# Talking-heads attention and two MoE layers on one core: pre-mix and post-mix as matmuls in two array halves of 64 columns

## The chip, the core and the metric

The kernel runs on one NeuronCore of one Trainium2 chip. Its engines work side by side, each through its own instruction stream: PE (TensorE) multiplies, with its weight loads shown as PEld; DVE (VectorE), ACT (ScalarE) and POOL (GpSimd) work element by element; SP (SyncE) only issues DMAs. The metric is the device time of one execution in microseconds. A **record** is one PE instruction in the trace: a float32 matmul of this kernel leaves two records, each with a weight load of its own.

## The reference, cut to what matters

```python
# q, k, v: (4, 12, 448, 64); w_pre, w_post: (12, 12)
scores = scale * np.matmul(q, k.transpose(0, 1, 3, 2))
scores = np.einsum('bhij,hg->bgij', scores, w_pre)          # pre-mix over heads
scores = scores - np.max(scores, axis=-1, keepdims=True)
attn = np.exp(scores)
attn = attn / (np.sum(attn, axis=-1, keepdims=True) + 1e-09)
attn = np.einsum('bhij,hg->bgij', attn, w_post)             # post-mix over heads
attn_out = np.matmul(attn, v)                               # AV
x = attn_out.transpose(0, 2, 1, 3).reshape(1792, 768)
# two MoE layers follow: 768 -> 1024 (SoLU and a norm) -> 768, then 768 -> 2048 (ReLU squared) -> 768
```

## The kernel before, in words

The attention takes each of the 4 batches in 4 chunks of queries (120, 120, 120 and 88). Each chunk is cut into blocks of at most 10 queries (R = 10), 180 blocks in all. With 12 heads a block has up to 120 (query, head) rows, and these are the partitions on which the mixes over heads work:

- `qk` (L199) makes the scores of one chunk, a third of the heads at a time, with 64 contracted rows in either row half of the array, and writes them to `ssrc`.
- `shuffle` (L214) is a DMA that lays the scores of a block out as 120 (query, head) rows by 448 keys, `sdst`.
- `pre` (L226) is the pre-mix: one matmul of a 120x120 block-diagonal matrix `wpre_bd` with the 448 columns of `sdst`. `negmax` (DVE, L239) and `expo` (ACT, L251) follow.
- `weigh` (every second block) turns the sums into `w`: DVE adds and takes the reciprocal (L260, L262), POOL multiplies the block-diagonal post weights by it (L268). For the last 14 blocks ACT does this (L275).
- `post` (L288) is the post-mix: for each of 4 pieces of 112 keys one matmul with `e` (120x112) as weights and `w` (120 columns) streaming. It turns the block so that keys are the partitions. `post_out` (DVE, L302) copies the 480 elements per partition to `at`.
- `av` (L315) runs once for a finished chunk: for 6 pairs of heads and 4 pieces of keys, two matmuls with 64 weight columns, one for each head, which write to PSUM partitions 0 to 63 and 64 to 127: the two column halves of the array. ACT copies the result to `xt` (L325, L330); `x_out` (L340) stores it.

The order on every engine is written out by hand: one loop over slots `s`, one slot for a block, issues `shuffle(s+8)`, `pre(s+3)`, `post_out(s-1)`, `weigh(s+1)`, `negmax` and `expo(s+3)`, any `qk` and `av` that is due, and last `post(s)`. So PE's order in a slot is pre, qk or av if there is one, post. Other work is spread over the slots: splitting q and k into high and low parts, narrowing the first MoE weights (`filler`), and late in the attention the loads for the first MoE layer (`prep_first`) and four pieces of its first matmuls (L419). The MoE layers that follow are untouched by the change.

## Time and profile before

| | |
|---|---|
| device time, 3 executions | 1178.35, 1180.03 and 1181.02 us; median 1180.03 us |
| profiled execution's own time (its span, first to last instruction) | 1178.6 us |
| PE busy | 1168.5 us, 99% |
| PE weight loads busy | 1021.1 us, 87% |
| DVE, ACT, POOL busy | 744.8, 490.9, 279.8 us |
| granted TensorE clock | 1.00 over the whole span (the upper level, 2.4 GHz) |

PE counts as busy from the start of a record to its modelled end, and the records overlap in the array, so a busy PE says little by itself. What a matmul costs is read from the distance between the starts of neighbouring rows in the timeline.

### The profile page before, as it was taken

How to read it: one execution, taken by the hardware profiler on the slowest of the kernel's cores; microseconds unless marked ns; L12 is line 12 of the kernel's file. 1: busy time of each engine (PE TensorE's matmuls, PEld its weight loads, DVE VectorE, ACT ScalarE, POOL GpSimd, SP SyncE). 2: the span in 40 equal slices, each digit the busy share in tenths (PEclk: the TensorE clock that was granted, in tenths of full speed). 3: DMA queues.
4: the chain of work that ended last, by engine and by line, in shares of the span. 5: the costliest groups of instructions: out<-in, count | busy, mean ns of one | idle time of the engine just before them, and what ended most of it. 6: DMA issues, size and time to landing. Idle time of an engine off the chain costs nothing.

```text
span 1178.6 us, 21505 instructions
## 1 busy us (share of the span) xinstructions
PE 1168.5 (99%) x8034; PEld 1021.1 (87%) x8034; DVE 744.8 (63%) x1480; ACT 490.9 (42%) x1206; POOL 279.8 (24%) x386
## 2 busy tenths in 40 slices
PE   9999999999999999999999999999999999999998
PEld 4777777777777768899899999999999999999998
DVE  4776777677777664853354378457676767676734
ACT  4556555666666554422122146533232222222211
POOL 2342223223322161730110074211111111111100
PEclk9999999999999999999999999999999999999999
DMA  6875766566656452411110265212121212121113
GB/s 178 215 200 166 224 185 193 164 216 202 185 179 195 137 172 86 121 48 48 54 41 27 70 200 173 69 41 64 45 62 46 65 44 63 45 66 43 41 68 121
DMA packets 103267, 134.40 MB, mean 114 GB/s; under 512 B 21499, under 2 KB 86395, under 8 KB 103163
## 3 DMA queue, kind: packets, MB, share of 16 engines
q1 hardware_dynamic: 102379, 132.75, 37.7%
q8 instruction: 64, 1.05, 0.4%
q14 instruction: 40, 0.33, 0.1%
q10 hardware_dynamic: 784, 0.27, 0.1%
HBM read 71.65 MB, written 22.81 MB: 80 GB/s over the span
## 4 chain that ended last, share of the span: by engine, by line
PE 91%; DVE 2%; DMA 2%; ACT 1%; issue 1%; POOL 1%; SPq 0%; POOLq 0%; DVEq 0%; ACTq 0%
PE ps_y L885 19%; PE ps_h L846 19%; PE ps_post L288 12%; PE ps_pre L226 10%; PE ps_h L419 10%; PE ps_o L692 8%; PE ps_av L315 6%; PE ps_qk L199 6%; PE ps_tr L678 1%; DMA x2r<-x2D 1%; DMA wraw<-w1iD 1%; DMA wr<-in_moe_w_out_dram 1%; DVE nm L239 1%; DVE at L302 0%; ACT e L251 0%
## 5 line engine op out<-in xcount | busy, mean ns | idle before, releaser
L846 PE MATMUL ps_h<-x,ti 128*128 128x384 f32 (+1 forms) x1440 | 241.6, 325 | 0.0
L885 PE MATMUL ps_y<-to,g 128*128 128x384 f32 x1332 | 239.3, 336 | 1.1 <-ACT y L894 1.1
L846 PEld LDWEIGHTS ps_h<-x,ti 128*128 128x128 f32 x1440 | 236.6, 188 | 0.0
L885 PEld LDWEIGHTS ps_y<-to,g 128*128 128x128 f32 x1332 | 231.0, 188 | 3.4 <-DVE y L896 1.9
L288 PEld LDWEIGHTS ps_post<-w,e 120*112 120x112 f32 (+1 forms) x1440 | 168.3, 177 | 68.4 <-issue 48.2
L302 DVE COPY at<-ps_post 112x480 f32<-112x480 f32 x180 | 117.3, 652 | 109.4 <-PE ps_post L288 108.9
L288 PE MATMUL ps_post<-w,e 120*112 120x120 f32 (+1 forms) x1440 | 182.7, 270 | 2.6 <-ACT w L275 2.1
L251 ACT ACTIVATE e<-ps_pre,nm 120x448 f32<-120x448 f32 x180 | 114.6, 637 | 132.0 <-POOL w L268 73.3
L226 PE MATMUL ps_pre<-sdst,wpre_bd 120*120 120x448 f32 x360 | 166.3, 545 | 0.8 <-ACT e L251 0.7
L854 ACT ACTIVATE r<-ps_h 128x384 f32<-128x384 f32 (+1 forms) x80 | 37.4, 468 | 213.1 <-PE ps_h L846 213.1
L692 PE MATMUL ps_o<-zt,w1o 128*128 128x384 f32 (+1 forms) x720 | 120.1, 326 | 0.0
L419 PE MATMUL ps_h<-w1i,xs 128*128 128x512 f32 x504 | 119.2, 393 | 0.4 <-ACT xt L330 0.4
L855 DVE SCALAR_TENSOR_TENSOR r<-ps_h,r 128x384 f32<-128x384 f32 (+1 forms) x80 | 42.4, 531 | 121.7 <-ACT r L854 121.7
L692 PEld LDWEIGHTS ps_o<-zt,w1o 128*128 128x128 f32 x720 | 117.0, 189 | 0.0
L239 DVE TENSOR_REDUCE nm<-ps_pre 120x1 f32<-120x448 f32 x180 | 110.2, 613 | 7.9 <-PE ps_pre L226 5.3
L896 DVE TENSOR_TENSOR y<-ps_y,y 128x768 f32<-128x768 f32 x97 | 92.4, 953 | 31.2 <-PE ps_y L885 31.2
L419 PEld LDWEIGHTS ps_h<-w1i,xs 128*128 128x128 f32 x504 | 93.9, 188 | 19.9 <-ACT xt L330 0.6
L268 POOL TENSOR_TENSOR w<-wpost_bd,sm 120x120 f32<-120x120 f32 x166 | 64.1, 406 | 188.1 <-DVE sm L262 176.8
L208 ACT COPY ssrc<-ps_qk 120x448 f32<-120x448 f32 (+1 forms) x186 | 84.9, 543 | 10.0 <-PE ps_qk L199 10.0
L315 PEld LDWEIGHTS ps_av<-at,v 112*64 112x64 f32 x1536 | 73.8, 137 | 11.4 <-ACT ssrc L208 5.3
L802 POOL TENSOR_TENSOR ti<-wt,ti 128x384 fp32r<-128x384 f32 x32 | 34.7, 1085 | 205.4 <-ACT ti L801 205.3
L315 PE MATMUL ps_av<-at,v 112*64 112x120 f32 (+1 forms) x1536 | 78.0, 261 | 0.4 <-ACT xt L325 0.3
(79 smaller groups left out, 1168.1 us busy)
## 6 DMA issues: line engine op xcount, KB each, us to landing
sdst<-ssrc SPq DMA_DIRECT2D x172, 210.0 KB
wr<-in_moe_w_in_dram SPq DMA_DIRECT2D x32, 384.0 KB
wr<-in_moe_w_out_dram SPq DMA_DIRECT2D x32, 384.0 KB
w1raw<-in_moe_w_in_dram SPq DMA_DIRECT2D x24, 256.0 KB
w1raw<-in_moe_w_out_dram SPq DMA_DIRECT2D x24, 256.0 KB
kraw<-in_kT_dram SPq DMA_DIRECT2D x24, 224.0 KB
v<-in_v_dram SPq DMA_DIRECT2D x16, 336.0 KB
out_dram<-y SPq DMA_DIRECT2D x13, 384.0 KB
```

The costliest lines, as they stand in the source:

```text
L208: (nc.vector.tensor_copy if dve else nc.scalar.copy)(ssrc[c][0:n, h, :], ps[0:n, 0:S])
L226: nc.tensor.matmul(out=ps[0:m, 0:S], lhsT=wpre_bd[0:m].rearrange("p i g -> p (i g)")[:, 0:m], rhs=d[0:m], start=True, stop=True,)
L239: nc.vector.tensor_reduce(out=nm[0:m], in_=ps[0:m, 0:S], op=ALU.max, axis=AX.X, negate=True)
L251: nc.scalar.activation(out=e[0:m], in_=ps[0:m, 0:S], func=AF.Exp, bias=nm[0:m], scale=1.0, accum_out=sm[0:m])
L288: nc.tensor.matmul(out=ps[:, j, :, 0:r], lhsT=e[0:m, j * JW:(j + 1) * JW], rhs=w[0:m, :, 0:r], start=True, stop=True,)
L302: nc.vector.tensor_copy(at[c][:, :, :, oa:oa + r], ps[:, :, :, 0:r])
L315: nc.tensor.matmul(out=ps[64 * e:64 * e + 64, 0:n], lhsT=vv[ch["b"], j][:, 2 * p + e], rhs=a[:, j, 2 * p + e, 0:n], start=(j == 0), stop=( ...
L419: nc.tensor.matmul(out=ps[:, u], lhsT=t[:, a, cc], rhs=w1i[cc][:, w, u * 512:(u + 1) * 512], start=(cc == 0 and a == 0 and w == 0), stop=( ...
L692: nc.tensor.matmul(out=ps[:, 0:width], lhsT=w1o[k][:, w, cc * 128:(cc + 1) * 128], rhs=zT[:, a, k, 0:width], start=(k == 0 and i == 0), st ...
L846: nc.tensor.matmul(out=ps[:, 0:n], lhsT=ti[:, w, cc, f * 128:(f + 1) * 128], rhs=x2[q][:, a, cc], start=(cc == 0 and i == 0), stop=(cc == ...
L885: nc.tensor.matmul(out=ps[:, u - us[0], 0:DM // 2], lhsT=g[:, a, f, o:o + 128], rhs=to[:, w, f, u * (DM // 2):(u + 1) * (DM // 2)], start= ...
L896: nc.vector.tensor_tensor(out=yo, in0=po, in1=yo, op=ALU.add)
```

## The change

The pre-mix is now eight matmuls for a block: four pieces of 112 keys (QP), each once for the first and once for the second half of the block's queries, with 64 weight columns (60 of them used) and results in PSUM partitions 0 to 63 or 64 to 127. So the 120 rows of a block lie on 128 partitions with a gap of 4 in each half, and `negmax`, `expo` and `weigh` work on 128 partitions. The post-mix cuts the keys into pieces of 64: three pairs of pieces, each piece in its own column half against all 120 columns of `w`, and a last piece of 64 keys that both halves take, one with heads 0 to 5, the other with heads 6 to 11 (60 columns each). `at` therefore holds 420 elements per partition for a block of ten queries, not 480. AV keeps its 8 matmuls for a pair of heads, now heads p and p+6. Its last piece contracts over 128 partitions that hold the same 64 keys twice, for either head, against a tile of V in which the other head's half is zero; POOL sets these zeros. The loads of V, the store of `xt` and the constants follow the new layout.

```diff
@@ -41,8 +41,14 @@
     R = 10
-    JW = 112
+    JW = 128
     NJ = S // JW
+    JL = S - NJ * JW
+    G2 = H // 2
+    NU = NJ * H + G2
+    RH = R // 2
+    PR = RH * H
+    QP = 112
...
     mask_sb = const.tile([120, R], F32, name="mask_sb")
-    wp_raw = const.tile([120, 2, H], F32, name="wp_raw")
-    wpre_bd = const.tile([120, R, H], F32, name="wpre_bd")
-    wpost_bd = const.tile([120, H, R], F32, name="wpost_bd")
+    mask_gap = const.tile([128, R], F32, name="mask_gap")
+    wp_raw = const.tile([120, H], F32, name="wp_raw")
+    wq_raw = const.tile([128, H], F32, name="wq_raw")
+    wpre_bd = const.tile([120, 2, 64], F32, name="wpre_bd")
+    wpost_bd = const.tile([128, H, R], F32, name="wpost_bd")
...
     def load_v(b, j):
-        t = late_p.tile([JW, H, D], F32, tag=f"v_{j}", name="v", bufs=2)
-        nc.sync.dma_start(out=t, in_=v[b, j * JW:(j + 1) * JW].rearrange("j (g d) -> j g d", g=H))
+        if j < NJ:
+            t = late_p.tile([JW, H, D], F32, tag=f"v_{j}", name="v", bufs=2)
+            nc.sync.dma_start(out=t, in_=v[b, j * JW:(j + 1) * JW].rearrange("j (g d) -> j g d", g=H))
+        else:
+            t = late_p.tile([128, 2, G2, D], F32, tag=f"v_{j}", name="v", bufs=2)
+            src = v[b, j * JW:S].rearrange("j (e g d) -> e j g d", e=2, g=G2)
+            for e in range(2):
+                nc.gpsimd.memset(t[64 - 64 * e:128 - 64 * e, e], 0.0)
+            for e in range(2):
+                nc.sync.dma_start(out=t[64 * e:64 * e + 64, e], in_=src[e])
         vv[b, j] = t
 
...
@@ -223,56 +239,50 @@
         m = blocks[t][2] * H
         d = sdst.pop(t)
         ps = psb_p.tile([128, 512], F32, tag="pre", name="ps_pre", bufs=2)
-        nc.tensor.matmul(
-            out=ps[0:m, 0:S],
-            lhsT=wpre_bd[0:m].rearrange("p i g -> p (i g)")[:, 0:m],
-            rhs=d[0:m],
-            start=True,
-            stop=True,
-        )
+        for o in range(0, S, QP):
+            for u in range(2):
+                nc.tensor.matmul(
+                    out=ps[64 * u:64 * u + 64, o:o + QP],
+                    lhsT=wpre_bd[0:m, u],
+                    rhs=d[0:m, o:o + QP],
+                    start=True,
+                    stop=True,
+                )
         pres[t] = ps
...
     def expo(t):
-        m = blocks[t][2] * H
         ps, nm = pres.pop(t)
-        e = late_p.tile([120, S], F32, tag="e", name="e", bufs=4)
+        e = late_p.tile([128, S], F32, tag="e", name="e", bufs=4)
         if t % 2 == 0:
-            sms[t] = late_p.tile([120, 2], F32, tag="sm", name="sm", bufs=4)
-            if m < 120 or blocks[t + 1][2] < R:
-                nc.vector.memset(sms[t], 1.0)
+            sms[t] = late_p.tile([128, 2], F32, tag="sm", name="sm", bufs=4)
         sm = sms[t - t % 2][:, t % 2:t % 2 + 1]
-        nc.scalar.activation(
-            out=e[0:m], in_=ps[0:m, 0:S], func=AF.Exp, bias=nm[0:m], scale=1.0, accum_out=sm[0:m]
-        )
+        nc.scalar.activation(out=e, in_=ps[:, 0:S], func=AF.Exp, bias=nm, scale=1.0, accum_out=sm)
         es[t] = e
...
     def weigh(t):
 
-        m = max(blocks[u][2] for u in (t, t + 1)) * H
         sm = sms.pop(t)
-        nc.vector.tensor_scalar(out=sm[0:m], in0=sm[0:m], scalar1=1e-9, scalar2=None, op0=ALU.add)
+        nc.vector.tensor_scalar(out=sm, in0=sm, scalar1=1e-9, scalar2=None, op0=ALU.add)
...
-            m = blocks[t + u][2] * H
-            w = late_p.tile([120, H, R], F32, tag="w", name="w", bufs=4)
+            w = late_p.tile([128, H, R], F32, tag="w", name="w", bufs=4)
             if t < tail:
                 nc.gpsimd.tensor_tensor(
-                    out=w[0:m].rearrange("p g i -> p (g i)"),
-                    in0=wpost_bd[0:m].rearrange("p g i -> p (g i)"),
-                    in1=sm[0:m, u:u + 1].to_broadcast([m, H * R]),
+                    out=w.rearrange("p g i -> p (g i)"),
+                    in0=wpost_bd.rearrange("p g i -> p (g i)"),
+                    in1=sm[:, u:u + 1].to_broadcast([128, H * R]),
                     op=ALU.mult,
                 )
             else:
-                nc.scalar.activation(out=w[0:m], in_=wpost_bd[0:m], func=AF.Copy, scale=sm[0:m, u:u + 1])
+                nc.scalar.activation(out=w, in_=wpost_bd, func=AF.Copy, scale=sm[:, u:u + 1])
...
 
     def post(t):
         r = blocks[t][2]
-        m = r * H
         e, w = es.pop(t), ws.pop(t)
-        ps = psa_p.tile([JW, NJ, H, R], F32, tag="post", name="ps_post", bufs=2)
-        for j in range(NJ):
-            nc.tensor.matmul(
-                out=ps[:, j, :, 0:r],
-                lhsT=e[0:m, j * JW:(j + 1) * JW],
-                rhs=w[0:m, :, 0:r],
-                start=True,
-                stop=True,
-            )
+        ps = psa_p.tile([128, NU, R], F32, tag="post", name="ps_post", bufs=2)
+        for j in range(NJ + 1):
+            for u in range(2):
+                o = j * JW + u * 64 if j < NJ else NJ * JW
+                g0, ng = (0, H) if j < NJ else (u * G2, G2)
+                nc.tensor.matmul(
+                    out=ps[64 * u:64 * u + 64, j * H:j * H + ng, 0:r],
+                    lhsT=e[:, o:o + 64],
+                    rhs=w[:, g0:g0 + ng, 0:r],
+                    start=True,
+                    stop=True,
+                )
         pps[t] = ps
 
     def post_out(t):
         c, k, r, oa = blocks[t]
         ps = pps.pop(t)
         if c not in at:
-            at[c] = late_p.tile([JW, NJ, H, 120], F32, tag="at", name="at", bufs=2)
-        nc.vector.tensor_copy(at[c][:, :, :, oa:oa + r], ps[:, :, :, 0:r])
+            at[c] = late_p.tile([128, NU, 120], F32, tag="at", name="at", bufs=2)
+        nc.vector.tensor_copy(at[c][:, :, oa:oa + r], ps[:, :, 0:r])
...
         ps = pool.tile([128, 512], F32, tag=tag, name="ps_av", bufs=bufs)
-        for j in range(NJ):
+        for j in range(NJ + 1):
+            t = vv[ch["b"], j]
             for e in range(2):
+                g = p + e * G2
                 nc.tensor.matmul(
                     out=ps[64 * e:64 * e + 64, 0:n],
-                    lhsT=vv[ch["b"], j][:, 2 * p + e],
-                    rhs=a[:, j, 2 * p + e, 0:n],
+                    lhsT=t[:, g] if j < NJ else t[:, e, p],
+                    rhs=a[:, j * H + (g if j < NJ else p), 0:n],
                     start=(j == 0),
-                    stop=(j == NJ - 1),
+                    stop=(j == NJ),
                 )
...
     def x_out(c, eng=nc.sync):
         ch = chunks[c]
         t0, n = ch["b"] * S + ch["i0"], ch["n"]
-        eng.dma_start(
-            out=xD[:, t0:t0 + n].rearrange("(c p) t -> p c t", p=128),
-            in_=xt.pop(c)[:, :, 0:n],
-        )
+        x = xt.pop(c)
+        for e in range(2):
+            eng.dma_start(
+                out=xD[e * G2 * D:(e + 1) * G2 * D, t0:t0 + n].rearrange("(c d) t -> d c t", d=D),
+                in_=x[64 * e:64 * e + 64, :, 0:n],
+            )
...
+    nc.gpsimd.memset(mask_gap, 0.0)
+    nc.gpsimd.memset(wq_raw, 0.0)
+    nc.gpsimd.memset(wpre_bd, 0.0)
     nc.sync.dma_start(out=mask_sb, in_=mask)
-    for u, w in enumerate((w_pre, w_post)):
-        nc.sync.dma_start(out=wp_raw[:, u, :], in_=w.unsqueeze(0).to_broadcast([R, H, H]))
+    nc.sync.dma_start(out=wp_raw, in_=w_pre.unsqueeze(0).to_broadcast([R, H, H]))
     load_q(1)
+    for u in range(2):
+        nc.sync.dma_start(out=mask_gap[64 * u:64 * u + PR], in_=mask[u * PR:(u + 1) * PR])
+        nc.sync.dma_start(out=wq_raw[64 * u:64 * u + PR], in_=w_post.unsqueeze(0).to_broadcast([RH, H, H]))
 
...
-        )
+        nc.vector.tensor_scalar(out=wp_raw, in0=wp_raw, scalar1=scale, scalar2=None, op0=ALU.mult)
+        for u in range(2):
+            nc.vector.tensor_tensor(
+                out=wpre_bd[:, u, 0:PR].rearrange("p (i g) -> p i g", g=H),
+                in0=wp_raw.unsqueeze(1).to_broadcast([120, RH, H]),
+                in1=mask_sb[:, u * RH:(u + 1) * RH].unsqueeze(2).to_broadcast([120, RH, H]),
+                op=ALU.mult,
+            )
         nc.vector.tensor_tensor(
             out=wpost_bd,
-            in0=wp_raw[:, 1, :].unsqueeze(2).to_broadcast([120, H, R]),
-            in1=mask_sb.unsqueeze(1).to_broadcast([120, H, R]),
+            in0=wq_raw.unsqueeze(2).to_broadcast([128, H, R]),
+            in1=mask_gap.unsqueeze(1).to_broadcast([128, H, R]),
             op=ALU.mult,
...
     for c, ch in enumerate(chunks):
         if ch["i0"] == 0:
-            for j in range(NJ):
+            for j in range(NJ + 1):
                 at_slot(ch["first"] + ([6, 8, 10, 12] if c == 0 else [0, 2, 4, 6])[j], load_v, ch["b"], j)
```

On PE, early in the attention, around the `av` of the first chunk. Before, the rows are (x4 means four matmuls in a row):

```order
L199 MATMUL ps_qk<-k,q 120x448 x12
L288 MATMUL ps_post<-w,e 112x120 x4
L226 MATMUL ps_pre<-sdst,wpre_bd 120x448
L288 MATMUL ps_post<-w,e 112x120 x4
L226 MATMUL ps_pre<-sdst,wpre_bd 120x448
L315 MATMUL ps_av<-at,v 64x120 x48
L288 MATMUL ps_post<-w,e 112x120 x4
```

At the same place on PE in the changed kernel:

```order
L215 MATMUL ps_qk<-k,q 120x448 x12
L300 MATMUL ps_post<-w,e 64x120 x6
L300 MATMUL ps_post<-w,e 64x60 x2
L244 MATMUL ps_pre<-sdst,wpre_bd 64x112 x8
L300 MATMUL ps_post<-w,e 64x120 x6
L300 MATMUL ps_post<-w,e 64x60 x2
L244 MATMUL ps_pre<-sdst,wpre_bd 64x112 x8
L329 MATMUL ps_av<-at,v 64x120 x48
L300 MATMUL ps_post<-w,e 64x120 x6
```

The sequence of steps is the same. A block's mixes are 16 matmuls where they were 5, each with 64 weight columns as in AV; qk and AV are the same matmuls as before.

On SP, from the start of the program, where the inputs are loaded. Before:

```order
L166 DMA qraw<-in_qT_dram 64x720 x2
L149 DMA kraw<-in_kT_dram 64x2x448 x6
L449 DMA mask_sb<-in_mask_dram 120x10
L451 DMA wp_raw<-in_w_pre_dram 120x1x12
L451 DMA wp_raw<-in_w_post_dram 120x1x12
L166 DMA qraw<-in_qT_dram 64x720 x2
L214 DMA sdst<-ssrc 120x1x448 x2
```

The same place on SP after the change:

```order
L174 DMA qraw<-in_qT_dram 64x720 x2
L157 DMA kraw<-in_kT_dram 64x2x448 x6
L468 DMA mask_sb<-in_mask_dram 120x10
L469 DMA wp_raw<-in_w_pre_dram 120x1x12
L174 DMA qraw<-in_qT_dram 64x720 x2
L472 DMA mask_gap<-in_mask_dram 60x10
L473 DMA wq_raw<-in_w_post_dram 60x1x12
L472 DMA mask_gap<-in_mask_dram 60x10
L473 DMA wq_raw<-in_w_post_dram 60x1x12
L230 DMA sdst<-ssrc 120x1x448 x2
```

One small load in front of the second load of q is gone, and four small ones stand behind it, ahead of the first shuffle.

On POOL, in the second batch, in the changed kernel (w is the weighted post matrix, v the last piece of V, k and q the splits):

```order
L278 TENSOR_TENSOR w<-wpost_bd,sm 128x120 x4
L194 MEMSET v 64x384 x2
L278 TENSOR_TENSOR w<-wpost_bd,sm 128x120 x6
L184 TENSOR_TENSOR q<-qraw,q 128x264
L278 TENSOR_TENSOR w<-wpost_bd,sm 128x120 x2
```

The two MEMSET rows are new, once in each of the 4 batches; the rows around them stand as before.

## Rows read from the trace of the kernel before

**Rows 1.** The page: engine totals, granted clock in 40 slices, chain that ended last.

```profile
PE 1168.5 (99%) x8034; PEld 1021.1 (87%) x8034; DVE 744.8 (63%) x1480; ACT 490.9 (42%) x1206; POOL 279.8 (24%) x386
...
PEclk9999999999999999999999999999999999999999
...
PE 91%; DVE 2%; DMA 2%; ACT 1%; issue 1%; POOL 1%; SPq 0%; POOLq 0%; DVEq 0%; ACTq 0%
```

**Rows 2.** Windows: us, busy us (instructions) of each engine, clock, DMA share, GB/s.

```profile
24.00:406.00 382.00, 381.37 (x3325) 282.78 (x3325) 276.91 (x720) 234.48 (x652) 112.21 (x208) 1.00 0.64 190
...
432.00:466.00 34.00, 32.65 (x332) 26.52 (x330) 16.37 (x40) 15.56 (x54) 11.53 (x16) 1.00 0.44 133
466.00:1179.00 713.00, 708.02 (x4084) 684.68 (x4084) 426.62 (x663) 215.67 (x438) 139.81 (x133) 1.00 0.23 69
```

**Rows 3.** Timeline of PE from 300 us: start, us, line, records, idle before.

```profile
300.65 0.92 PE L226 MATMUL ps_pre<-sdst,wpre_bd 120*120 120x448 f32 x2
301.50 5.14 PE L315 MATMUL ps_av<-at,v 112*64 112x120 f32 x96
306.57 1.07 PE L288 MATMUL ps_post<-w,e 120*112 120x120 f32 x8
307.48 0.92 PE L226 MATMUL ps_pre<-sdst,wpre_bd 120*120 120x448 f32 x2
308.24 0.98 PE L288 MATMUL ps_post<-w,e 120*112 120x120 f32 x8
309.06 0.92 PE L226 MATMUL ps_pre<-sdst,wpre_bd 120*120 120x448 f32 x2
309.90 1.46 PE L199 MATMUL ps_qk<-k,q 64*120 64x448 f32 x12
311.30 1.07 PE L288 MATMUL ps_post<-w,e 120*112 120x120 f32 x8
312.21 0.92 PE L226 MATMUL ps_pre<-sdst,wpre_bd 120*120 120x448 f32 x2
```

**Rows 4.** Timeline of ACT: copies of finished AV head pairs, chunk of 120 queries.

```profile
305.05 0.37 ACT L325 COPY xt<-ps_av 128x120 f32<-128x120 f32 x1 [0.45 <-PE ps_av L315]
305.87 0.37 ACT L325 COPY xt<-ps_av 128x120 f32<-128x120 f32 x1 [0.45 <-PE ps_av L315]
```

**Rows 5.** The same for a chunk of 88 queries.

```profile
136.60 0.29 ACT L325 COPY xt<-ps_av 128x70 f32<-128x70 f32 x1 [0.29 <-PE ps_av L315]
...
137.21 0.28 ACT L325 COPY xt<-ps_av 128x70 f32<-128x70 f32 x1 [0.29 <-PE ps_av L315]
```

**Rows 6.** The page's groups: xcount, busy us, mean ns, idle before and its releaser.

```profile
L302 DVE COPY at<-ps_post 112x480 f32<-112x480 f32 x180 | 117.3, 652 | 109.4 <-PE ps_post L288 108.9
L288 PE MATMUL ps_post<-w,e 120*112 120x120 f32 (+1 forms) x1440 | 182.7, 270 | 2.6 <-ACT w L275 2.1
...
L226 PE MATMUL ps_pre<-sdst,wpre_bd 120*120 120x448 f32 x360 | 166.3, 545 | 0.8 <-ACT e L251 0.7
```

**Rows 7.** Timeline of PE late in the attention.

```profile
434.40 1.07 PE L288 MATMUL ps_post<-w,e 120*112 120x120 f32 x8 [0.61 <-ACT w L275]
435.24 1.63 PE L419 MATMUL ps_h<-w1i,xs 128*128 128x512 f32 x6
436.71 0.92 PE L226 MATMUL ps_pre<-sdst,wpre_bd 120*120 120x448 f32 x2
```

**Rows 8.** Waits, whole span: who for whom, us in total, times, longest.

```profile
PEld ps_post L288 <- POOL w L268: 12.5, 34, 0.9
```

**Rows 9.** Timeline of the start: POOL and SP.

```profile
0.73 0.31 POOL L438 MEMSET wz<- 128x256 f32 x1 [0.29 <-POOLq L968]
...
6.66 0.90 SPq L451 DMA_DIRECT2D wp_raw<-in_w_pre_dram  x1
...
13.75 1.73 SPq L214 DMA_DIRECT2D sdst<-ssrc  x2
```

**Rows 10.** The page's DMA queues: packets, MB, share of 16 engines.

```profile
q8 instruction: 64, 1.05, 0.4%
```

15 lines of the change are left out of this document (3 added, 12 removed).

## Prediction, made before the changed kernel had run

> **What bounds the kernel now.** I read the page first, for the one engine that is never idle; then the windows, to cut the span into stretches; then PE's timeline inside the attention, because the page's busy time counts overlapping records. The page gives PE 99% of the span, the chain that ended last runs through PE for 91% of it, and the clock is at its upper level in every slice [rows 1]. In the windows the attention's steady part, 24 to 406 us, has PE busy for 381.4 of 382 us while DVE has 277, ACT 234 and POOL 112; after 466 us come the MoE layers, which the change does not touch [rows 2]. In PE's timeline the reader is to look at distances between starts: a post-mix takes 0.82 us (308.24 to 309.06), a pre-mix 0.76 (307.48 to 308.24), and the next step begins at once [rows 3]. PE's waits for data are 2.6 us before all post-mixes and 0.8 before all pre-mixes [rows 6]. So up to about 430 us the attention is as long as the sum of PE's steps, and a shorter step should shorten the span.
>
> There are 180 blocks [rows 6]. The sum below is made against the profiled execution's 1178.6 us; the median of the three runs is 1.4 us above that, and I add this at the end.
>
> **What a matmul in a column half costs.** The trace of before holds this form already, in AV: two halves of 64 weight columns. ACT's copies show when each pair of heads is done, and a pair of heads is 8 matmuls, 16 records, that is 8 times two records side by side. With 120 streaming columns a pair of heads takes 0.82 us (305.05 to 305.87) [rows 4], so two records side by side take 0.1025 us; a full-width post-mix record of the same 120 columns takes as long alone (0.82 us for 8 records) [rows 3]. With 88 columns it is 0.61 us, 0.076 us for two side by side [rows 5]. Between 88 and 120 columns the cost follows the columns (0.026 us for 32 of them, 0.83 ns each), so neither loading of weights nor issue shows at 88.
>
> **Post-mix.** It was 8 records, 0.82 us. Now there are three pairs of pieces with 120 columns: 6 times two records side by side, 0.615 us. The last piece has 60 columns, 2 times two records. By columns alone one such pair is 0.076 less 28 times 0.83 ns, 0.053 us. It can't be cheaper than that; if the 0.076 us at 88 columns is already the floor, it is 0.076. A weight load of 64 columns lies close by: after AV, where the first load can't be done ahead, the post-mix takes 0.91 instead of 0.82 us (306.57 to 307.48) [rows 3], 0.09 us for 112 columns, so about 0.052 for 64. I take 0.055, close to the columns' side, since at 88 the columns still rule. The post-mix is then 0.615 + 0.11 = 0.725 us, 0.095 less; times 180, **-17.1 us** (bounds -17.6 and -9.5).
>
> **Pre-mix.** It was 0.76 us by the row; its two records of 448 columns, at 0.83 ns each as below 120 columns in AV, would be 0.747; I take 0.755. Now 16 records of 112 columns, 8 times two side by side, each between the two AV rows: 0.076 + 24 times 0.83 ns = 0.096, in all 0.768 us. 0.013 more; times 180, **+2.3 us** (from 0 to +5, if the first records of each block don't close up). That both halves stream the same rows, where AV's stream different ones, no row shows; it is a rival below.
>
> **The changes of mode around AV.** Entering AV from the pre-mix costs 0.85 (300.65 to 301.50) where 0.755 is streaming: 0.09. AV takes 5.07 us (301.50 to 306.57) for 48 times 0.1025 = 4.92: 0.15. The post-mix behind it takes 0.91 for 0.82: 0.09 [rows 3]. Now pre-mix, AV and post-mix all work in the same two halves, and the three should vanish: 0.33 us at 15 of the 16 chunks (the last AV is followed by the MoE's matmuls), **-5.0 us** (0 if something else than the mode makes the gap).
>
> **The changes around qk** stay: qk still splits the array by rows. Only the load that lies open behind it is shorter, 64 columns for 112: the post-mix from 311.30 takes 0.91 [rows 3], and of its 0.09 us 0.04 goes. Of the 48 qk groups the three of the first chunk stand before any mix and two more run into another step; 43 stand ahead of a post-mix: **-1.7 us**. Four pieces of MoE matmuls (L419, full width) stand among the last blocks; today they follow without a seam (434.40 to 435.24, 0.84 us) [rows 7]. Each now gets two changes, about 0.19 going in and 0.15 coming out, by the seams above: **+1.5 us**.
>
> **What is hidden, and behind what.** The copy to `at` on DVE goes from 480 to 420 elements; it is 652 ns and its engine waits 108.9 us in all for the post-mix [rows 6]: a gain without effect. Two zero fills of 64x384 on POOL in each batch: the start's fill of 128x256 took 0.31 us [rows 9], so about 0.5 each, on an engine that is busy for 112 of 382 us [rows 2]. Behind them on POOL stand the products `w`, for which the post-mix waits; uncovered, all eight would cost 4 us, and I count nothing, since they wait for no new data and can run in POOL's idle time. SP gets a net of three small loads at the start: up to 0.90 us each, 2.7 us of issue. From the end of the row at 6.66 to the first shuffle at 13.75 the old queue has 6.2 us for three loads [rows 9]; six fit as well, so nothing. Later it gets one more issue for each store of `xt` and each last piece of V, again under 0.90 us each, on a queue that runs 8 slots ahead. The zero-padded piece of V leaves AV its 96 records.
>
> **What is given back.** The other engines don't get faster by what PE gains, save for the copy. 34 times a post-mix's weight load ends its wait by POOL's `w` [rows 8], and 14 blocks at the end wait for ACT's `w` (0.61 us of idle at 434.40) [rows 7]. In those 14 the 0.083 us of net gain is lost, 1.2 us; for the others I set 34 times 0.04. Together **+2.5 us** (0 to 5). What is late next is `w`: post-mix to copy to sums to POOL to the post-mix two slots on.
>
> **Sum:** -17.1 + 2.3 - 5.0 - 1.7 + 1.5 + 2.5 = -17.5. 1178.6 - 17.5 = 1161.1, and with 1.4 for the median **1162.5 us**, 1.5% faster. Its own range: all good ends (-22.8) give 1157, all bad ones except for the switches (-9.5 + 5 - 5 - 1.7 + 1.5 + 5 = -4.7) 1175; not all come together, so 1156, with a microsecond of the runs' own spread, to 1170.
>
> **A rule that speaks against it.** A block's mixes are 32 records and 32 loads now, for 10 and 10 (two records for each matmul) [rows 6]. AV with 88 columns ran 96 records at 0.038 us each [rows 5]. The Trainium skill (TensorE: Matmul & The Clock Gate, Wait — 56ns, not 53.3ns?) says that with hardware decode off the sequencer spends about 62 ns on each matmul, which then binds. By it a block would need 32 times 0.062 = 1.98 us, an estimate from that page, where the rows give 1.49, and the kernel would be some 70 us slower than before; the trace's 0.038 us does not agree.
>
> **The rivals.**
> *Instructions come too slowly (slower).* AV's rate was held for only 96 records, between stretches of long matmuls; now it is to be held for the whole attention. Before, 64 fetches of instructions bring 1.05 MB in all [rows 10]; the mixes' records grow from 1800 to 5760, so PE's 8034 matmul records [rows 1] become about half as many again. It decides where a record costs more on average than 1.575 / 32 = 0.049 us: at 0.055 a block is 1.76 us, +0.185 times 180 = +33 us, less 5 for the switches: about 1208. Against it: 0.038 in the 88-column AV. The page's rule above would be this rival with a higher price. 6 in 100.
> *The halves don't run side by side when both read the same columns (slower).* Alone, each record takes its own columns' time: pre-mix 1.53 us, post-mix 1.45, together +1.4 us for a block, about 1430. Against it: AV, the same form with other operands. 3 in 100.
> *Half the gain is lost* to a last piece at 0.076 (+7.6 us) or to `w` and exp coming too late in most short slots (another +5): 1168 to 1176. For it: DVE's share of 277 in 382 us; against it: the 2.6 us of waits. 17 in 100.
> *No change that can be told:* all mode switches remain and the last piece is at its floor, with waits: 1176 to 1182. 5 in 100.
>
> **How the numbers follow.** The forecast has 69 in 100 at 1156 to 1168. A measurement of this kernel can tell 0.2% (2.4 us) from nothing. Faster by more: 69 + 17 and a part of the fourth, 0.87; within: 0.04; slower: 0.09. From 1156 up, 80 in 100 are reached with two thirds of the half-lost case, to 1172.
>
> **What would show it.** In PE's timeline of the changed kernel a post-mix start is 0.72 to 0.73 us ahead of the next pre-mix, a pre-mix 0.77 ahead of the next post-mix; AV's distance to its neighbours is 0.77 in and 4.92 across, with no longer post-mix behind it; the first MoE matmuls then start some 17 us earlier than 466 us less what the last blocks wait. Wrong it would be with PE records of 60 columns spaced as those of 88, with mixes whose two halves start one behind the other, or with PE's idle time before L300 in tens of microseconds.

## The result, and the profile after

The changed kernel takes **1167.61 us** (median of 4 executions, 1165.94 to 1168.66); the kernel before takes 1179.45 (4 executions) beside it. The ratio is 0.9899, 95% interval 0.9885 to 0.9913: 11.8 us or 1.0% faster, where 17.5 us were forecast, inside the range of 1156 to 1172 and 5.1 us above the forecast itself. The profiled execution's span is 1165.1 us, 13.5 below the 1178.6 of before.

The page of the changed kernel, with the lines that answer to [rows 1, 6, 10] (busy us and count of records; then the clock, the fetches of instructions, and groups with count, busy us, mean ns, idle before):

```profile
PE 1152.9 (99%) x11994; PEld 1084.9 (93%) x11994; DVE 738.1 (63%) x1475; ACT 490.6 (42%) x1206; POOL 283.7 (24%) x397
...
PEclk9999999999999999999999999999999999999999
...
q8 instruction: 95, 1.56, 0.5%
...
L244 PE MATMUL ps_pre<-sdst,wpre_bd 120*64 120x112 f32 (+1 forms) x2880 | 170.7, 261 | 1.4 <-ACT e L265 1.2
...
L300 PE MATMUL ps_post<-w,e 128*64 128x120 f32 (+2 forms) x2880 | 163.8, 256 | 3.2 <-ACT w L285 2.2
...
L314 DVE COPY at<-ps_post 128x420 f32<-128x420 f32 x180 | 105.7, 587 | 92.7 <-PE ps_post L300 91.6
```

PE runs half as many records again, at the same upper clock, and DVE's copy is 65 ns shorter. The page's idle columns hide most of what follows: since the end of a PE record is modelled, a wait of a tenth of a microsecond between two steps leaves no gap. So the steps are read from their starts.

PE's timeline of the changed kernel, around an AV of 120 columns (to be set against [rows 3]) and at one of 88 (start, us, line, records, idle before):

```profile
290.87 0.94 PE L244 MATMUL ps_pre<-sdst,wpre_bd 120*64 120x112 f32 x16
291.65 5.09 PE L329 MATMUL ps_av<-at,v 128*64 128x120 f32 x96
296.57 0.90 PE L300 MATMUL ps_post<-w,e 128*64 128x120 f32 x16
297.30 0.94 PE L244 MATMUL ps_pre<-sdst,wpre_bd 120*64 120x112 f32 x16
298.07 0.90 PE L300 MATMUL ps_post<-w,e 128*64 128x120 f32 x16
298.80 0.94 PE L244 MATMUL ps_pre<-sdst,wpre_bd 120*64 120x112 f32 x16
299.67 1.47 PE L215 MATMUL ps_qk<-k,q 64*120 64x448 f32 x12
301.07 0.95 PE L300 MATMUL ps_post<-w,e 128*64 128x120 f32 x16
301.85 0.94 PE L244 MATMUL ps_pre<-sdst,wpre_bd 120*64 120x112 f32 x16
...
342.92 2.60 PE L329 MATMUL ps_av<-at,v 128*64 128x88 f32 x64
345.93 1.43 PE L329 MATMUL ps_av<-at,v 128*64 128x88 f32 x32 [0.41 <-ACT xt L344]
347.19 0.90 PE L300 MATMUL ps_post<-w,e 128*64 128x120 f32 x16
```

A post-mix now takes 0.73 us (297.30 less 296.57; 0.82 before), a pre-mix 0.77 (298.07 less 297.30; 0.76 before). AV is entered 0.78 us after the pre-mix's start (0.85), is left after 4.92 (5.07), and the post-mix behind it is no longer than any other (0.91 before). Behind qk it takes 0.78 (0.91). The step behind qk was priced in the prediction's part on qk, the others stand in its last part. The last rows show what does not: an AV that stops for ACT's copies after two thirds of its records.

**Steps and waits.** To separate the two, I took each PE step of the attention (from the start of a pre, post, qk or AV to the start of the next step), grouped the steps by kind, neighbours and size, and called what exceeds a group's usual length (its median; for the few AVs of 88 columns the undisturbed length) a wait. What is left is the length of the attention if PE never waited. For both kernels, in us:

| | before | after | |
|---|---|---|---|
| attention, first post-mix to the row behind the last AV | 442.0 | 428.1 | -13.9 |
| of it steps | 434.6 | 416.1 | -18.5 |
| of it waits | 7.4 | 12.0 | +4.6 |
| waits in the pre-mix's step, for the next post-mix's `w` above all | 4.9 | 6.1 | +1.2 |
| waits in the post-mix's step, for the next pre-mix (exp) above all | 1.3 | 3.1 | +1.8 |
| waits inside AV, for ACT's copies to `xt` | 1.2 | 2.7 | +1.5 |

So the whole difference lies in the attention, the steps give 18.5 us, and in these two executions a quarter of that comes back as waits, spread over three kinds. By the medians more is lost: 11.8 of the 18.5 us arrive. Each figure of waits is that of one execution, and the times of one kernel's runs lie 1.2 to 4.6 us apart, so a difference of a microsecond between two kernels' waits proves little.

Where the waits stand tells more than their kinds. In the steady part, up to the last qk, they double, from about 3.6 to 7.5 us (+1.4 in the pre-mix's step, +1.8 in the post-mix's, +0.7 inside AV). In the last part behind it, where PE's longest waits are, they hardly change: 3.7 and 4.5. There DVE, ACT and POOL also split the weights of the first MoE layer. From the timelines of DVE, ACT and PE in the changed kernel, at the longest wait of all:

```profile
414.58 0.17 DVE L273 RECIPROCAL sm<-sm 128x2 f32<-128x2 f32 x1
415.42 0.40 ACT L422 CAST w1i<-wraw 128x256 fp32r<-128x256 f32 x1 [1.81 <-DMA wraw<-w1iD]
415.73 0.68 ACT L285 ACTIVATE w<-wpost_bd,sm 128x120 f32<-128x120 f32 x2
416.17 0.95 PE L300 MATMUL ps_post<-w,e 128*64 128x120 f32 x16 [1.39 <-ACT w L285]
```

The sums are ready at 414.75, but `w` stands on ACT behind a cast (part of the split) that has waited 1.81 us for a DMA with those weights, and starts at 415.73. ACT's timeline of the kernel before has the same, ahead of PE's longest wait for `w` there (1.18 us, at 430.31):

```profile
429.56 0.40 ACT L406 CAST w1i<-wraw 128x256 fp32r<-128x256 f32 x1 [1.89 <-DMA wraw<-w1iD]
```

### The profile page after: what moved, and what is told of

It reads as the page before. It is cut to its first block, busy times and chain, and to the rows that moved or that the text cites. A ratio compares the mean times of both kernels' runs of the same rounds, so it can differ in the third digit from the quotient of the medians.

```text
span 1165.1 us, 29455 instructions
## 1 busy us (share of the span) xinstructions
PE 1152.9 (99%) x11994; PEld 1084.9 (93%) x11994; DVE 738.1 (63%) x1475; ACT 490.6 (42%) x1206; POOL 283.7 (24%) x397
## 3 DMA queue, kind: packets, MB, share of 16 engines
q8 instruction: 95, 1.56, 0.5%
## 4 chain that ended last, share of the span: by engine, by line
PE 90%; DVE 3%; ACT 3%; DMA 2%; issue 1%; POOL 0%; ACTq 0%; SPq 0%; POOLq 0%; DVEq 0%
PE ps_y L905 20%; PE ps_h L866 20%; PE ps_o L712 10%; PE ps_h L435 9%; PE ps_post L300 9%; PE ps_pre L244 9%; PE ps_av L329 6%; PE ps_qk L215 5%; ACT e L265 1%; PE ps_tr L698 1%; DVE nm L256 1%; ACT ssrc L224 1%; DMA sdst<-ssrc 1%; PE ps_pre L460 1%; DMA wraw<-w1iD 1%
## 5 line engine op out<-in xcount | busy, mean ns | idle before, releaser
L244 PE MATMUL ps_pre<-sdst,wpre_bd 120*64 120x112 f32 (+1 forms) x2880 | 170.7, 261 | 1.4 <-ACT e L265 1.2
L300 PEld LDWEIGHTS ps_post<-w,e 128*64 128x64 f32 x2880 | 151.2, 137 | 20.1 <-issue 10.6
L300 PE MATMUL ps_post<-w,e 128*64 128x120 f32 (+2 forms) x2880 | 163.8, 256 | 3.2 <-ACT w L285 2.2
L265 ACT ACTIVATE e<-ps_pre,nm 128x448 f32<-128x448 f32 x180 | 114.6, 637 | 120.3 <-POOL w L278 78.2
L314 DVE COPY at<-ps_post 128x420 f32<-128x420 f32 x180 | 105.7, 587 | 92.7 <-PE ps_post L300 91.6
L244 PEld LDWEIGHTS ps_pre<-sdst,wpre_bd 120*64 120x64 f32 (+1 forms) x2880 | 140.1, 137 | 4.4 <-ACT e L265 2.3
L256 DVE TENSOR_REDUCE nm<-ps_pre 128x1 f32<-128x448 f32 x180 | 110.1, 612 | 9.0 <-PE ps_pre L244 8.7
L278 POOL TENSOR_TENSOR w<-wpost_bd,sm 128x120 f32<-128x120 f32 x166 | 64.1, 406 | 174.6 <-DVE sm L273 163.4
L329 PE MATMUL ps_av<-at,v 128*64 128x120 f32 (+1 forms) x1536 | 77.7, 260 | 1.7 <-ACT xt L339 1.0
```

Source lines behind the costliest of these rows:

```text
L244: nc.tensor.matmul(out=ps[64 * u:64 * u + 64, o:o + QP], lhsT=wpre_bd[0:m, u], rhs=d[0:m, o:o + QP], start=True, stop=True,)
L256: nc.vector.tensor_reduce(out=nm, in_=ps[:, 0:S], op=ALU.max, axis=AX.X, negate=True)
L265: nc.scalar.activation(out=e, in_=ps[:, 0:S], func=AF.Exp, bias=nm, scale=1.0, accum_out=sm)
L300: nc.tensor.matmul(out=ps[64 * u:64 * u + 64, j * H:j * H + ng, 0:r], lhsT=e[:, o:o + 64], rhs=w[:, g0:g0 + ng, 0:r], start=True, stop=True,)
L314: nc.vector.tensor_copy(at[c][:, :, oa:oa + r], ps[:, :, 0:r])
L329: nc.tensor.matmul(out=ps[64 * e:64 * e + 64, 0:n], lhsT=t[:, g] if j < NJ else t[:, e, p], rhs=a[:, j * H + (g if j < NJ else p), 0:n], s ...
```

## The experiments

The theory was that PE's steps cost what was forecast and that the rest is waits, made by the chain of copy, sums and `w` on a crowded DVE. The rivals: that the seams or the short records are mispriced, and that no single chain makes the waits, so that room given to one is used up by the next. Late loads in the last part, which the rows above show, were not among the theories, and no experiment was made for them. Every kernel is compared with runs of the kernel before on the same chip; "waits" is the quantity of the table, from the kernel's profiled execution.

**1. The fillers moved.** Around one early wait (PE's post-mix at 170.95 us) DVE's filler work (the narrowing of weights, 0.41 us at 169.78) stands between the sums and the reciprocal, in the chain to `w`. The edit puts it behind the maximum and the exponential:

```diff
         nc.vector.tensor_scalar(out=sm, in0=sm, scalar1=1e-9, scalar2=None, op0=ALU.add)
-        filler()
         nc.vector.reciprocal(sm, sm)
-        filler()
...
             weigh(s + 1)
-        else:
-            filler()
         if 0 <= s + DP < NB:
             negmax(s + DP)
             expo(s + DP)
+        for _ in range(2 if 0 <= s + 1 < NB and (s + 1) % 2 == 0 else 1):
+            filler()
```

> The changed kernel with one thing moved on DVE: the filler pieces (narrowing of MoE weights) that stood inside weigh and ahead of negmax now stand behind negmax and expo, so that the sums, w and the row maximum no longer queue behind 0.4 us pieces. Theory A (PE's steps became as short as forecast, and the missing 4 to 6 us are waits of PE for w, for exp and for ACT's copies of AV, all fed by DVE): 3 to 6 us faster than the changed kernel, about 1162 to 1165 us, and the rows of PE that wait for POOL's w and ACT's e in the steady part mostly gone. Theory B (the missing part lies elsewhere, in the start, the last blocks or the MoE layers): within 1.5 us of the changed kernel's 1167.6.

Measured: 1175.5 us (1173.84 to 1178.43), ratio 0.9971 [0.9962, 0.9981]: 8 us slower than the change alone. Waits grow from 12.0 to 18.2 us. The view of waits (who for whom, us in total, times, longest) of PE's matmuls from 24 to 450 us in this kernel:

```profile
PE ps_pre L244 <- ACT e L265: 4.1, 9, 0.9
PE ps_av L327 <- ACT xt L337: 2.6, 2, 2.1
PE ps_post L298 <- ACT w L283: 2.0, 2, 1.4
PE ps_av L327 <- ACT ssrc L224: 0.9, 1, 0.9
PE ps_post L298 <- POOL w L276: 0.2, 1, 0.2
```

The wait for exp leads this list; the same view of the changed kernel has:

```profile
PE ps_pre L244 <- ACT e L265: 0.5, 3, 0.2
```

In the post-mix's steps the waits grow from 3.1 to 7.7 us, and in the pre-mix's, those for `w`, they do not fall (6.1 to 6.7). The cure failed. It does not clear the fillers: they left one place in DVE's order, and now stand ahead of the next block's copy and maximum, in the chains to the next `w` and exp.

**2. The last piece of the post-mix twice.** The same four records once more, into columns of PSUM that nobody reads; PE gets longer and no other engine does.

```diff
...
+        for u in range(2):
+            nc.tensor.matmul(
+                out=ps[64 * u:64 * u + 64, NJ * H + G2:NJ * H + H, 0:r],
+                lhsT=e[:, NJ * JW:S],
+                rhs=w[:, u * G2:u * G2 + G2, 0:r],
...
```

> The changed kernel with the last piece of the post-mix done twice (the second time into PSUM columns that nobody reads): 2 matmuls of 60 columns more in each block, by the trace after 0.106 us of PE, 19 us in all. If every microsecond of PE's steps arrives at the end, 1186 to 1187 us. Theory A (some of PE's gain went into waits) says that these waits give back what they took, so only 13 to 16 us arrive: 1180 to 1184 us. Theory B says the full 19.

Measured: 1182.65 us (1181.35 to 1183.87), ratio 1.0022 [1.0013, 1.0031], 15.0 more than the change. PE's timeline:

```profile
299.33 0.90 PE L300 MATMUL ps_post<-w,e 128*64 128x120 f32 x16
300.06 0.29 PE L308 MATMUL ps_post<-w,e 128*64 128x60 f32 x4
300.18 0.94 PE L244 MATMUL ps_pre<-sdst,wpre_bd 120*64 120x112 f32 x16
```

The added piece takes 0.12 us (300.06 to 300.18) for two times two records side by side, some 0.06 us for each two, close to the 0.055 of the prediction. The steps grow by 20.7 us (436.8 less 416.1), the waits fall from 12.0 to 6.4: a quarter of PE's work that is added here costs nothing (15.0 of 20.7 us arrive), as a quarter of what the change took away gave nothing in the profiled pair.

**3. The pre-mix undone.** One full-width matmul again, with the post-mix and AV left in halves:

```diff
-        for o in range(0, S, QP):
-            for u in range(2):
-                nc.tensor.matmul(
-                    out=ps[64 * u:64 * u + 64, o:o + QP],
-                    lhsT=wpre_bd[0:m, u],
-                    rhs=d[0:m, o:o + QP],
...
+        nc.tensor.matmul(
+            out=ps[:, 0:S],
+            lhsT=wpre_bd[0:m].rearrange("p u g -> p (u g)"),
+            rhs=d[0:m],
...
```

> The changed kernel with the pre-mix undone: one matmul over the full width with 128 weight columns (gaps included) and 448 streaming columns, the post-mix and AV still in halves. PE changes its mode twice in each block. From the seams read before the change (0.09 to get in or out, 0.05 to 0.10 for a first load that lies open) about 0.33 us for a block, less 0.018 that the pre-mix itself gains: 56 us of PE, of which some 5 are covered by waits that shrink: about 1215 to 1222 us. The rival (what looked like a change of mode at AV was a wait for data) gives 0.018 times 180 less than the changed kernel: 1164 us.

Measured: 1205.92 us (1205.59 to 1206.68), ratio 1.0224 [1.021, 1.0238], 38.3 more than the change. PE's timeline:

```profile
24.65 1.02 PE L242 MATMUL ps_pre<-sdst,wpre_bd 120*128 120x448 f32 x2
25.60 0.95 PE L298 MATMUL ps_post<-w,e 128*64 128x120 f32 x16
26.48 1.02 PE L242 MATMUL ps_pre<-sdst,wpre_bd 120*128 120x448 f32 x2
```

A short slot is 1.83 us (24.65 to 26.48) where the change has 1.50: 0.95 for the pre-mix, 0.88 for the post-mix. That is 0.33 us above the change's slot for going into halves and out again, or 0.35 when the full-width pre-mix is counted at its 0.755; the prediction read 0.33 around AV. The time came out below what was expected, since the waits fall from 12.0 to 1.2 us: 49.9 us of longer steps are paid with 39.1.

**4. The mirror: post-mix pieces at full width.** Three full-width matmuls for the pieces of 128 keys, the last piece still by heads in the halves:

```diff
+            if j < NJ:
+                nc.tensor.matmul(
+                    out=ps[:, j * H:j * H + H, 0:r],
+                    lhsT=e[:, j * JW:(j + 1) * JW],
+                    rhs=w[:, :, 0:r],
...
+                continue
...
```

> The mirror of the kernel with a full-width pre-mix: only the three 128-key pieces of the post-mix are undone, into three full-width matmuls with 128 weight columns; the last piece of 64 keys stays split by heads over the two halves, the pre-mix and AV stay in halves. By the rows, a full-width matmul of 120 columns takes as long as two half-width ones side by side, so streaming is the same, 0.725 us. Theory A (each change between full width and halves costs time, 0.33 us for a pair of changes, as the short slot of 1.83 us showed for the pre-mix): the short slot becomes about 1.83 us, less 12 us of covered waits: 1200 to 1215 us. Rival (the seam is special to long streams of the pre-mix; short records hide it): 1166 to 1172 us.

Measured: 1221.24 us (1220.8 to 1221.52), ratio 1.0353 [1.0338, 1.0367]; above what was expected. PE's timeline:

```profile
307.50 0.93 PE L298 MATMUL ps_post<-w,e 128*128 128x120 f32 x6
308.36 0.33 PE L309 MATMUL ps_post<-w,e 128*64 128x60 f32 x4
308.52 0.94 PE L244 MATMUL ps_pre<-sdst,wpre_bd 120*64 120x112 f32 x16
309.39 0.93 PE L298 MATMUL ps_post<-w,e 128*128 128x120 f32 x6
```

The short slot is 1.89 us (307.50 to 309.39), 0.39 above the change's: 0.86 for six records that stream 0.615, 0.16 for the last piece, 0.87 for the pre-mix. So a change of mode costs a little more here than with the pre-mix at full width, and short records hide none of it. The kernel loses 53.6 us, although it streams no more columns. Together the two experiments show that putting only one mix into halves would have lost time (the post-mix's last piece is still in halves here).

This kernel also shows that the mode, and not another form of its matmuls, shortened AV. In the changed kernel AV contracts over 128 rows, before over 112, so it is not quite the same; but with those 128 rows and a full-width post-mix behind it, AV takes 5.03 us again (4.92 in the change, 5.07 before):

```profile
295.41 5.09 PE L338 MATMUL ps_av<-at,v 128*64 128x120 f32 x96
300.44 0.93 PE L298 MATMUL ps_post<-w,e 128*128 128x120 f32 x6
```

**5. Pieces of 448 columns in the pre-mix.** One matmul for each half:

```diff
-    QP = 112
+    QP = 448
```

> The changed kernel with the pre-mix's halves in one piece of 448 columns each (2 matmuls for a block, 4 records) in place of four pieces of 112. If the two halves run side by side whatever the length, a block's pre-mix is 2 times 0.376 = 0.752 instead of 0.772 us, 3.6 us of PE in all, of which about two thirds arrive: 1165 us. If the halves need short pieces in turn because matmuls start in program order (both records of one half, then both of the other), half or all of the overlap goes: a pre-mix of 1.13 to 1.5 us, 1230 to 1300 us.

Measured: 1165.36 us (1164.76 to 1165.95), ratio 0.9879 [0.9864, 0.9895]; 2.3 below the change. PE's timeline:

```profile
295.31 0.90 PE L300 MATMUL ps_post<-w,e 128*64 128x120 f32 x16
296.03 0.93 PE L244 MATMUL ps_pre<-sdst,wpre_bd 120*64 120x448 f32 x4
296.79 0.90 PE L300 MATMUL ps_post<-w,e 128*64 128x120 f32 x16
```

The halves run side by side with long pieces too: 0.76 us (296.03 to 296.79), what a full-width pre-mix takes in [rows 3]. The short pieces cost 0.016 us a block (0.773 less 0.757 in the usual distances). The steps fall by 2.7 us against the change, and the waits rise by 1.2.

**6. Without the addition of 1e-9.** The reciprocal takes the addition's place, so the chain to `w` is shorter by one DVE step and by the filler that stood between the two; both fillers now follow the reciprocal, where the expectation has them in their old places. A row's sum holds the exponential of its maximum, which is 1, and beside that the addition disappears in float32. On the change, on the kernel before, and on the change with pieces of 448:

```diff
-        nc.vector.tensor_scalar(out=sm, in0=sm, scalar1=1e-9, scalar2=None, op0=ALU.add)
+        nc.vector.reciprocal(sm, sm)
         filler()
-        nc.vector.reciprocal(sm, sm)
         filler()
```

> The changed kernel without the addition of 1e-9 to the row sums (each sum holds exp(0) = 1, so in float32 the addition changes no bit): 90 small DVE instructions fewer, 22 us of DVE by the profile of before, and a step less between exp and w. The fillers keep their places around the reciprocal. Theory C (after the change DVE's queue in runs of slots without qk or AV sets when w and exp are ready, and PE waits for both): 3 to 5 us faster than the changed kernel, 1163 to 1165 us, with PE's waits for w and exp in the steady part about halved. Theory D (ACT's and POOL's own queues make them late, so that less work on DVE moves nothing): within 1 us of the changed kernel.

> The kernel before without that addition. Both theories: PE hardly waits there, so at most 1.5 us faster than before, 1178 to 1179.5 us. If it gains as much as the changed kernel does from the same edit, the waits are nothing that the change brought.

> The changed kernel without that addition and with the pre-mix's halves in one piece of 448 columns. The piece of 448 gave 2.3 us by itself. Theory C: the two add up to 5 to 7 us, 1160 to 1163 us. Theory D: only the 2.3 us of the pre-mix.

Measured: on the change 1166.84 us (1166.05 to 1169.87), ratio 0.9898 [0.9884, 0.9912], which can't be told from the change's; on the kernel before 1178.93, ratio 0.9997 [0.9988, 1.0006], nothing; with 448 columns 1165.05 (1164.12 to 1165.13), ratio 0.9878 [0.9863, 0.9893], what the 448 columns give alone. On the change and with 448 columns these are the times of theory D. In the profiled run with 448 columns the waits in the pre-mix's step, those for `w`, fall from 7.2 to 4.4 us against experiment 5, and those in the post-mix's step rise from 3.7 to 5.1: half of the room that a shorter chain gives is used up at the next wait.

The profiled run on the change alone is the longest of its four (1169.87 us), and it shows something else: the waits inside AV rise from 2.7 to 5.6 us by one AV. From the timelines of ACT and PE, and the row of the view of windows (us, then each engine's busy time, granted clock, DMA):

```profile
428.57 0.40 ACT L421 CAST w1i<-wraw 128x256 fp32r<-128x256 f32 x1 [3.55 <-DMA wraw<-w1iD]
...
430.47 5.17 PE L328 MATMUL ps_av<-at,v 128*64 128x120 f32 x64 [2.62 <-ACT xt L338]
...
430.83:434.23 3.40, 3.40 (x39) 3.40 (x37) 0.00 (x0) 0.74 (x2) 0.00 (x0) 0.50 0.00 0
```

ACT's copies stand behind a cast that waited 3.55 us for a DMA; PE stood still for 2.62 us, and soon after it went on the granted clock was 0.50, the lower level of 1.2 GHz, for 3.4 us. Part of what counts as a wait there is AV at that clock, and it says nothing of the chain that the edit shortened.

**7. Less filler on DVE.** Two of the four narrowing instructions are left out for every piece of the first MoE weights, so sign, exponent and low bits of those weights are missing:

```diff
-        yield from narrow(w1raw.pop(i), sq, t)
+        yield from narrow(w1raw.pop(i), sq, t, True)
...
-        nc.vector.scalar_tensor_tensor(
-            out=bits, in0=high, scalar=0xC0000000, in1=bits, op0=ALU.bitwise_and, op1=ALU.bitwise_or
-        )
+        if not less:
+            nc.vector.scalar_tensor_tensor(
+                out=bits, in0=high, scalar=0xC0000000, in1=bits, op0=ALU.bitwise_and, op1=ALU.bitwise_or
+            )
...
```

> The changed kernel with two of the four DVE instructions left out that narrow each piece of the first MoE layer's weights during the attention (sign, exponent and low bits stay out, so the MoE layers work on other numbers): 96 instructions of 0.42 us, 40 us of DVE spread over the attention; PE's work is unchanged. Theory C: PE's waits for w and exp go down to what they were before the change or lower, 4 to 7 us faster than the changed kernel: 1160 to 1164 us. Theory D: within 1.5 us of it.

Measured: 1165.04 us (1164.3 to 1165.73), ratio 0.9877 [0.9864, 0.9891], 2.6 below the change; between the two theories. In the profiled execution the attention ends 3.7 us earlier (448.05, not 451.76), close to the lower end of theory C's 4 to 7, and 1.6 of this is lost behind it, where the MoE layers work on other numbers. Waits fall from 12.0 to 8.6 us: in the post-mix's step from 3.1 to 1.3 (as before the change), in the pre-mix's from 6.1 to 4.6, inside AV hardly (2.7, 2.6). By place, those of the steady part go down from 7.5 to 3.5 us, as low as before the change (3.6), and 0.9 of the rest is one AV that waits for a load of V. Those of the last part, where no narrowing is left (its last piece is done at 379 us), stay: 4.5 and 5.1. So DVE's load is behind what the change added in the steady part, and not behind the last part.

**8. `w` on POOL to the end.** The kernel of experiment 5, in which POOL makes `w` for the last 14 blocks too:

```diff
-    tail = NB - 14
+    tail = NB
```

> The kernel with pieces of 448 columns in the pre-mix (1165.36 us), and w made on POOL for the last 14 blocks too, where the kernel before and after the change lets ACT make it. In the trace of that kernel the post-mix waits 3.0 us for ACT's w there, the largest wait that is left for one producer. Theory F (the wait hangs on the engine that makes w): 1162 to 1164 us. Theory D (the chain from copy and sums to w has no room at that place, whichever engine does its last step, and POOL has its splits of the MoE weights in front of it): 1164 to 1167 us, with waits for POOL's w in place of ACT's.

Measured: 1167.84 us (1167.14 to 1171.59), ratio 0.9906 [0.9893, 0.992], 2.5 above experiment 5. That is above the range of either theory. From the timelines of ACT, POOL and PE, at its longest wait:

```profile
415.59 0.40 ACT L422 CAST w1i<-wraw 128x256 fp32r<-128x256 f32 x1 [1.85 <-DMA wraw<-w1iD]
416.07 0.73 POOL L423 TENSOR_TENSOR w1i<-wraw,w1i 128x256 fp32r<-128x256 f32 x1 [1.47 <-ACT w1i L422]
416.76 0.72 POOL L278 TENSOR_TENSOR w<-wpost_bd,sm 128x120 f32<-128x120 f32 x2
417.20 0.95 PE L300 MATMUL ps_post<-w,e 128*64 128x120 f32 x16 [1.82 <-POOL w L278]
```

PE waits for POOL's `w` now; `w` stands behind a split of MoE weights, that split waits for ACT's cast, and the cast for its DMA. DVE had the sums ready at 414.22. All waits together grow from 13.2 to 15.2 us. So the edit changed the engine and kept what `w` queues behind there, a load of MoE weights that comes late. No run moved these loads, so their part in the time is read from rows and not shown by an experiment.

**9. The maximum first, around AV.** In the changed kernel's stop at 345.93 us the chain runs through two engines. ACT's timeline there:

```profile
343.09 0.66 ACT L265 ACTIVATE e<-ps_pre,nm 128x448 f32<-128x448 f32 x1
...
344.95 0.63 ACT L265 ACTIVATE e<-ps_pre,nm 128x448 f32<-128x448 f32 x1 [1.11 <-POOL w L278]
...
345.57 0.27 ACT L339 COPY xt<-ps_av 128x70 f32<-128x70 f32 x1
```

And DVE's:

```profile
343.94 0.17 DVE L271 TENSOR_SCALAR sm<-sm 128x2 f32<-128x2 f32 x1 [0.92 <-ACT e L265]
344.15 0.17 DVE L273 RECIPROCAL sm<-sm 128x2 f32<-128x2 f32 x1
344.23 0.60 DVE L256 TENSOR_REDUCE nm<-ps_pre 128x1 f32<-128x448 f32 x1
```

The sums wait for the exponential of 343.09, the maximum stands behind them on DVE, the next exponential waits for the maximum (the view names POOL's `w`; the maximum ended last, at 344.83), and ACT's copies of AV stand behind that, first at 345.57. AV has begun at 342.92, and after 64 records it needs a PSUM buffer back. None of these instructions got faster with the change. The edit, on the kernel of experiment 5:

```diff
+        early_max = 0 <= s + DP < NB and any(f is av for f, a in js)
+        if early_max:
+            negmax(s + DP)
+            expo(s + DP)
         if 0 <= s + 1 < NB and (s + 1) % 2 == 0:
             weigh(s + 1)
...
-        if 0 <= s + DP < NB:
+        if 0 <= s + DP < NB and not early_max:
```

> The kernel with pieces of 448 columns in the pre-mix (1165.36 us), with one order changed: in the 16 slots that hold an AV, the negated maximum and the exponential of the newest block are issued ahead of the sums of the older pair on DVE and ACT. In the changed kernel's trace AV of the 88-column chunks stops in its middle, since ACT's copies of AV stand behind an exponential, that behind DVE's maximum, and that behind sums which wait for the exponential before. Theory F (the order on DVE and ACT around AV makes these waits): AV's waits fall from 2.1 us to under 0.7, 1163 to 1164.5 us. Theory D (room taken from one chain is taken from the next): the w behind AV comes later and the time stays within 1 us of 1165.4.

Measured: 1165.87 us (1164.46 to 1166.94), ratio 0.9887 [0.987, 0.9903], no change against experiment 5. PE's timeline at the same AV:

```profile
342.02 3.81 PE L329 MATMUL ps_av<-at,v 128*64 128x88 f32 x96
345.67 0.90 PE L300 MATMUL ps_post<-w,e 128*64 128x120 f32 x16
```

It now runs through, in 3.65 us; three such AVs lose 0.0 us together where they lost 1.0. And yet the waits of the whole attention are 13.2 us as before: the pre-mix's and post-mix's steps wait 0.7 us longer in place of it, and the AVs of 120 columns 0.2.

**Steps against waits, all together** (us, attention of the profiled executions):

| kernel | steps | waits |
|---|---|---|
| post-mix pieces at full width (4) | 479.3 | 2.6 |
| pre-mix at full width (3) | 466.0 | 1.2 |
| last piece twice (2) | 436.8 | 6.4 |
| before | 434.6 | 7.4 |
| the change | 416.1 | 12.0 |
| pieces of 448 (5) | 413.5 | 13.2 |
| the same, maximum first (9) | 413.5 | 13.2 |
| the change with less filler (7) | 415.9 | 8.6 |

From before to the kernel with 448 columns the waits grow by 5.8 us as the steps fall by 21.1. Less work on DVE takes the waits off this course (experiment 7), and so does a worse order (experiment 1, 18.2).

## Why the prediction was right, and by what it was off

Direction and mechanism were right: PE's steps set the time, and they became as short as forecast. The size was not: the time lies 0.4 us inside the 1156 to 1168 that the forecast held most likely. The gain in the span is 4.0 us smaller than the sum of -17.5, and the median stands 1.1 us further above the profiled span than forecast (2.5, not 1.4). That 1.1 is no cost of the kernel: every run with a span on record takes 1.7 to 1.9 us more than its span, and the rest depends on which execution was profiled. Term by term, from the usual distances of PE's steps, in us:

| term of the sum | forecast | found |
|---|---|---|
| Post-mix | -17.1 | -16.6 (0.820 to 0.728, times 180) |
| Pre-mix | +2.3 | +3.7 (0.754 to 0.773, and 0.006 more ahead of 43 qk groups) |
| The changes of mode around AV | -5.0 | -5.0 (0.093 in, 0.149 across, 0.093 behind, times 15) |
| The changes around qk | -1.7 | -1.8 (0.911 to 0.777 behind qk, less the 0.092 of the post-mix) |
| MoE pieces among the last blocks | +1.5 | +1.2 (what is left of the -18.5) |
| What is given back | +2.5 | +4.6 (7.4 to 12.0) |
| outside the attention | 0 | +0.4 (-13.9 there, -13.5 in the span) |

- **What a matmul in a column half costs** carried over from AV to both mixes, with 60 columns on the side of the columns; experiment 2 measured that by itself at 0.06 us. The rival of halves one behind the other is out: it would have made the slot 2.98 us, and it is 1.50.
- **The rival of instructions that come too slowly** did not come about. A block's 32 records take 1.50 us, 0.047 us each, below the 0.049 from which that rival would have decided, while the fetches of instructions rise from 1.05 [rows 10] to 1.56 MB. The rule that the prediction weighed, some 62 ns of sequencer time for each matmul with hardware decode off (the Trainium skill, TensorE: Matmul & The Clock Gate, Wait — 56ns, not 53.3ns?), does not bind here either: this trace has 0.047 us for a record.
- **The mode switches**: experiments 3 and 4 put them back and measure 0.33 and 0.39 us a block. That a change of tiling mode drains the engine is what the Trainium skill says (TensorEngine Tiling (Array Packing), Key Properties); the trace fits it: it shows the time lost at each change, though not what the engine does in it.
- **The step that was mis-sized is "What is given back"**, 2.5 set and 4.6 found, near the upper bound of 5. The sum priced waits for `w` alone: 1.2 us for the last 14 blocks and 1.3 for all the others. In the last part the waits grew by 0.8; in the steady part by 3.9, for `w`, for exp and for ACT's copies in AV, and the last two have no price in the sum. The third rival did name a late exp, with another +5, and set the page's 2.6 us of waits against it; by the steps the kernel before already waited 7.4 us, for exp and inside AV too, of which the page's idle columns (2.6 and 0.8, [rows 6]) show a part. The wait at 434.40 [rows 7] that the prediction took for a late `w` has a late DMA in front of it too: ACT's cast ends its wait of 1.01 us for MoE weights at 433.65, and `w` follows at 433.96, with the sums ready since 433.12. The second miss is the pre-mix, at 3.7 of its bounds 0 to 5: its short pieces cost a little, as experiment 5 shows by doing without them.
- **Of the cause of the waits** the runs show this much: they grow as PE's steps shorten, whichever step it is (2 to 5), they move in part to another place when one chain is given room (6, 9) or get worse (1), and in the steady part they go back to what they were before the change when DVE has less to do (7). That is what a fixed order on each engine would give if DVE runs near PE's pace in many slots; how much belongs to ACT's and to POOL's order there was not settled. For the last part the rows name loads of MoE weights that come late, before and after the change; no experiment tests it. A wait of 0.83 us for DVE that the changed kernel's profile shows in the first MoE layer (PE at 461.46 us) was not followed; the span outside the attention grew by 0.4 us in all.

The fastest kernels here that still compute the reference are the change with pieces of 448 columns (1165.36) and the same without the addition (1165.05); both lie some 2 us below the change, with intervals of the ratios that overlap its own.
